# Clustered attention and experts on one core: q and k split one group sooner, masks in the order of the maxima, maxima of the second and third pair sooner

## The chip, the core and the metric

The kernel runs on one core of one Trainium2 chip. TensorE (PE in the profile) multiplies matrices, VectorE (DVE), ScalarE (ACT) and GpSimd (POOL) work on tiles, and SyncE (SP) issues nearly all DMAs. Each engine takes its own instructions in order and waits on semaphores for the others. The metric is the device time of one execution in microseconds.

## What is computed

Attention over 4 batches and 8 heads, 768 rows of 64 numbers each. Rows of q and k see each other only where their nearest of 16 centroids is the same. The result, as rows of 512 numbers, then goes through eight experts, one for each row that passes a gate.

```python
q_assign = np.argmax(np.einsum('bhsd,hcd->bhsc', q_n, c_n), axis=-1)
k_assign = np.argmax(np.einsum('bhsd,hcd->bhsc', k_n, c_n), axis=-1)
mask = q_assign[:, :, :, None] == k_assign[:, :, None, :]
scores = scale * np.matmul(q, k.transpose(0, 1, 3, 2))
scores = np.where(mask, scores, -1000000000.0)
scores = scores - np.max(scores, axis=-1, keepdims=True)
attn = np.exp(scores)
attn = attn / (np.sum(attn, axis=-1, keepdims=True) + 1e-09)
...
do_compute = skip_score > 0
xc = x[do_compute]
...
    h = np.maximum(xc[mask] @ w1[e], 0.0)
    y[mask] = gate_w[mask, None] * (h @ w2[e])
out[do_compute] = xc + y
```

## The kernel before

**Pairs and slots.** The attention works on 16 pairs of heads, one after the other. A pair has 24 slots: in each, `score` multiplies 128 rows of k with 384 rows of q for one of the two heads (a = 0 or 1) in two matmuls (L560 and L561), and ACT takes the exp into a ring of tiles PT (L563). A slot is the unit of time of the plan; slot 0 is the first product of a pair, and negative numbers lie in the pairs before it. Every six slots (a group) the products with v follow on PE (`avs`, tile av, L585). After the second group of six in each half, oT takes the result out of av, which has one buffer (L607 and L608 for the first half).

**Two precisions.** q and k are split into a high part and a low rest. `split_hi` writes the high part of q (t = 0) or k (t = 1) on ACT into a tile hi (L378; two such tiles in all, q's and k's) and copies it by DMA into QM (q) or KB (k), one for each head, three sets in turn (L381). `split_lo` subtracts it from raw, in place, on DVE (L388). `copies_hi` (L396) and `copies_lo` (L402) copy high and low parts into qc and kc, two sets in turn, for the second matmul.

**Masks.** `sims` (L438) multiplies raw with the centroids, `assign` picks the best centroid in five DVE operations on mxc, eqc, mwc and oh (L451 to L462), and `masks` turns oh into rows mk (L485) that eight small DMAs write into QM and KB below the high parts (L493): t for q or k, a for the head, hf for the half of 384 columns.

**Maxima.** Before a pair's products can start, each row's maximum is needed. `smax` runs 24 times for a pair: a matmul sm of QM and KB with their masks (L522), and a maximum on DVE into M (L524). n = 0 to 5 are head 0 of the first half of q, with both halves of k in turn; 6 to 11 are head 1; 12 to 23 the second half of q. `mneg` takes the maximum over M into MX (L535), and `mrows` turns MX on PE (L543) and writes it into QM as a row (L548).

**The order.** `steps` takes all steps of all pairs from one heap by their slot numbers and writes the instructions in that order; it sets the order on each engine's queue, not times. The numbers stand in PLAN, with FIRST in place of it for pairs 0, 1 and 2. `hi` and `lo` have two numbers, for q and k; `copies` has one for the high parts and one each for the low parts of q and k; `load` fetches raw (two buffers); `smax` is the first number, the step, and the gap between the halves (and a step for the second half where it differs); `oT` is the delay behind the last product with v of a half. A group counts six slots, so a number that falls by 6 goes one group forward, while all numbers 24 apart are at the same place of successive pairs.

**What else uses the queues.** SP also loads v (vt, L356), writes out the attention (`put_out`, out<-x, L668, behind the ACT rows of L676), and brings pieces of the experts' weights (wraw, L1040) during pairs 3 to 6. `sums`, `recip` and the routing are on PE, ACT and DVE between the slots. POOL adds up the exps (acc, L574).

Of the kernel before, what the change touches and what calls it, by code (L numbers as in the profile page):

```python
# [12 lines left out]
F32 = mybir.dt.float32  # L13
# [10 lines left out]
H, S, D, NCL = 8, 768, 64, 16  # L24
HP = H // 2
HALF = S // 2
# [17 lines left out]


PLAN = {
    "load": -54.0, "load_v": -45.0, "weights": 72.0, "sims": -42.9, "assign": (-42.45, 0.07, 0.02, 2.0, 0.02, 0.02),
    "hi": (-34.3, -28.3), "masks": (-34.5, 0.12), "lo": (-28.35, -10.35), "copies": (-23.3, -23.2, -10.3),
    "smax": (-21.1, 1.0, -0.4), "mneg": (-9.0, 3.2), "mrows": ((-4.5, 0.2, 0.05), (5.5, 0.1, 0.05)),
    "av": 1.6, "oT": (4.5, 3.55), "sums": 29.2, "recip": 31.5, "xout": (31.52, 49.55, 37.55),  # L50
    "tail": ((16.0, 16.6, 19.2), (28.5, 28.6, 29.3)),
    "route": (29.25, 34.9, 58.9), "early": (86.5, 100.9),
    "rtail": ((5.3, 10.9, 16.2, 17.5, 21.5, 18.2, 23.6, 24.2), (5.35, 10.92, 29.1, 29.2, 29.4, 29.5)),
# [6 lines left out]
FIRST = {  # L60
    0: {
        "load_v": -18.9, "sims": -20.0, "hi": (-19.9, -19.8, -19.7, -19.6), "assign": (-19.0, 0.1, 0.01, 0.01, 0.01, 0.01),
        "lo": (-18.7, -18.6, -16.9, -16.8), "masks": -17.0, "smax": (-14.0, 0.1, 13.0, 0.6), "mneg": (-12.85, 7.55),
        "mrows": ((-12.8, 0.1, 0.0), (8.2, 0.1, 0.0)),
    },
    1: {
        "sims": -42.2, "hi": (-42.4, -42.3), "lo": (-40.1, -40.0), "copies": (-39.9, -39.8, -39.7), "assign": (-36.83, 13.2, 1.3, 1.3, 1.3, 1.3),
        "masks": (-17.6, 0.1), "smax": (-14.5, 1.0, 0.0, 0.92), "mneg": (-2.3, 8.2), "mrows": ((-1.6, 0.1, 0.2), (8.8, 0.3, 0.3)),
    },
    2: {  # L70
        "load": -64.75, "smax": (-16.0, 0.95, 0.0), "mneg": (-5.2, 6.3), "mrows": ((-4.5, 0.2, 0.05), (7.4, 0.3, 0.3)),
    },
}

# [3 lines left out]
class Kernel:  # L78
# [397 lines left out]
    def masks(self, i, wait):  # L476

        c, nc = self.st[i], self.nc
        mp = self.xps([P, HALF])
        for b in range(NB):  # L480
            nc.tensor.matmul(mp[:, b * P:(b + 1) * P], lhsT=c["oh"][:, b].rearrange("p t h x -> p (t h x)"),
                             rhs=self.ident_bf, start=True, stop=True)
        yield wait
        mk = self.small.tile([P, HALF], F32R, name="mk", bufs=1)
        nc.scalar.activation(out=mk, in_=mp, func=AF.Identity, scale=self.mscale, bias=self.mbias)  # L485
        yield 0.3
        for t in range(2):
            for a in range(2):
                r = 64 + NCL * a
                for hf in range(2):  # L490
                    m0 = 64 * t + 32 * hf + NCL * a
                    dst = (c["kb"] if t else c["qm"])[a][r:r + NCL, hf * HALF:(hf + 1) * HALF]
                    nc.sync.dma_start(out=dst.bitcast(F32), in_=mk.bitcast(F32)[m0:m0 + NCL, :])  # L493

    def mask_rows(self, i, t, hf, mp):
        for b in range(NB):
# [842 lines left out]
```

## Time and profile before

| | |
|---|---|
| median of 3 runs | 740.55 us (735.31 to 742.02) |
| the profiled execution | 735.29 us, span of its instructions 733.6 us |
| attention ends, experts begin | near 505 us |
| TensorE clock granted, mean | 0.981 |
| DMAs moved | 110.16 MB, mean 150 GB/s |

The prediction quotes the profile. A line of waits has who waited and for whom, then us in total, times and the longest. A line of the timeline has start and duration in us, engine, line, operation, out<-in, the number of such instructions, and in brackets the engine's idle time before it with what ended it. A line of a stretch has its bounds and length, then for PE, PEld (weight loads), DVE, ACT and POOL the busy time with the number of instructions, then the granted share of the TensorE clock, the DMA share and GB/s. Tile names stand without their numbers, so QM is any of six. What ended a wait is inferred from semaphores; of several that a matmul waits for, the last is named.

### The profile page before, as it was taken

To read this page: it belongs to the slowest core of one execution; us is meant where nothing else is said; L and a number is where in the kernel's file an instruction comes from. 1 tells how busy PE (TensorE), PEld (TensorE's weight loads), DVE (VectorE), ACT (ScalarE), POOL (GpSimd) and SP (SyncE) were. 2 spreads that over 40 slices of the span, in tenths; PEclk is the share of its full clock that TensorE was granted. 3 is DMA by queue.
4 is the path that set the end of the run, shared out by engine and by line. 5 is a ranking of instruction groups with operands and counts; after the bars stand their busy time and mean duration, and the time that the engine had idled before them with its cause. 6 is when DMAs were issued, how large, how long until landed. Compare 5 with 4: busy or idle time off the path is not lost.

```text
span 733.6 us, 12354 instructions
## 1 busy us (share of the span) xinstructions
PE 675.4 (92%) x3961; PEld 472.0 (64%) x3961; DVE 499.8 (68%) x1022; ACT 425.7 (58%) x958; POOL 366.2 (50%) x390
## 2 busy tenths in 40 slices
PE   5798899999989989998999999998899999999995
PEld 2455556655656656565565656555578988998883
DVE  6856566757868757797675878776567876667711
ACT  6465657666656666775676757583454455455520
POOL 8664547756556665774665747642442222221001
PEclk9999999999999999999999999998799999999998
DMA  7643637575683663735646456140266666667520
GB/s 216 158 113 87 157 86 207 146 200 143 174 206 102 171 162 99 182 91 146 164 116 165 115 123 151 48 137 23 85 210 202 241 224 215 209 212 243 177 71 30
DMA packets 54353, 110.16 MB, mean 150 GB/s; under 512 B 8615, under 2 KB 22823, under 8 KB 54288
## 3 DMA queue, kind: packets, MB, share of 16 engines
q1 hardware_dynamic: 50832, 101.73, 49.9%
q0 software_dynamic: 2656, 7.24, 3.0%
q8 instruction: 32, 0.52, 0.3%
q10 hardware_dynamic: 800, 0.39, 0.2%
q14 instruction: 33, 0.27, 0.1%
HBM read 61.00 MB, written 10.62 MB: 98 GB/s over the span
## 4 chain that ended last, share of the span: by engine, by line
PE 57%; DMA 17%; issue 10%; DVE 4%; ACT 4%; POOL 3%; SPq 3%; POOLq 0%; ACTq 0%
PE av L585 13%; PE ps L560 9%; PE sm L522 8%; PE ps L561 7%; DMA out<-yo,idw 6%; DMA KB<-hi 5%; SPq L493 2%; DMA qc<-hi 2%; PE py L1070 2%; PE py L1071 2%; PE py L1072 2%; ACT PT L563 2%; DMA xg<-out,idr 2%; PE x_ps L438 2%; PE x_ps L617 2%
## 5 line engine op out<-in xcount | busy, mean ns | idle before, releaser
L574 POOL TENSOR_TENSOR acc<-acc,PT 128x384 f32<-128x384 f32 x248 | 239.7, 992 | 98.0 <-ACT PT L563 97.6
L563 ACT ACTIVATE PT<-ps 128x384 f32<-128x384 f32 x384 | 187.3, 492 | 148.8 <-PE ps L561 117.1
L524 DVE TENSOR_REDUCE M<-sm 128x1 f32<-128x384 f32 x384 | 204.2, 554 | 99.5 <-PE sm L522 98.1
L522 PE MATMUL sm<-KB,QM 96*128 96x384 f32 x384 | 138.8, 368 | 18.3 <-DMA KB<-hi 6.8
L560 PE MATMUL ps<-QM,KB 98*128 98x384 f32 x384 | 148.1, 386 | 2.8 <-ACT PT L563 1.5
L585 PE MATMUL av<-PT,vt 128*64 128x385 f32 x768 | 140.1, 500 | 3.9 <-ACT oT L608 3.9
L561 PE MATMUL ps<-qc,kc 128*128 128x384 f32 x384 | 132.3, 344 | 0.0
L560 PEld LDWEIGHTS ps<-QM,KB 98*128 98x128 f32 x384 | 73.3, 191 | 55.1 <-ACT PT L563 27.4
L522 PEld LDWEIGHTS sm<-KB,QM 96*128 96x128 f32 x384 | 75.1, 196 | 41.3 <-issue 29.2
L568 POOL TENSOR_TENSOR acc<-PT 128x384 f32<-128x384 f32 x64 | 54.3, 861 | 92.8 <-ACT PT L563 58.6
L585 PEld LDWEIGHTS av<-PT,vt 128*64 128x64 f32 x768 | 49.9, 137 | 62.2 <-issue 53.6
L966 POOL DMA_INDIRECT out<-yo,idw x15 | 19.3, 1286 | 113.5 <-DVE yo L1094 102.3
L561 PEld LDWEIGHTS ps<-qc,kc 128*128 128x128 f32 x384 | 74.3, 194 | 0.0
L1070 PE MATMUL ph<-x2l,w1h 128*128 128x256 f32 x224 | 63.6, 284 | 1.6 <-DVE x2l L1082 1.6
L1071 PE MATMUL ph<-x2h,w1h 128*128 128x256 f32 x224 | 63.6, 284 | 0.0
L1072 PE MATMUL ph<-x2h,w1l 128*128 128x256 f32 x224 | 63.5, 283 | 0.0
L1146 DVE SCALAR_TENSOR_TENSOR hl<-ph,hh 128x256 fp32r<-128x256 f32 x56 | 23.7, 423 | 38.6 <-ACT hh L1145 38.6
L1145 ACT ACTIVATE hh<-ph 128x256 fp32r<-128x256 f32 x56 | 21.5, 383 | 48.0 <-PE ph L1072 47.8
L676 ACT ACTIVATE x<-x_ps,rs 128x64 f32<-128x64 f32 x186 | 41.5, 323 | 11.2 <-DVE rs L633 7.1
L1070 PE MATMUL py<-w2l,hh 128*128 128x512 f32 x112 | 45.0, 402 | 0.0
L1070 PEld LDWEIGHTS ph<-x2l,w1h 128*128 128x128 f32 x224 | 42.9, 192 | 2.1 <-DVE x2l L1082 1.8
L1071 PE MATMUL py<-w2h,hh 128*128 128x512 f32 x112 | 43.7, 390 | 0.0
(262 smaller groups left out, 1007.2 us busy)
## 6 DMA issues: line engine op xcount, KB each, us to landing
wraw<-w SPq DMA_DIRECT2D x72, 512.0 KB, 4.6
raw<-qk SPq DMA_DIRECT2D x16, 768.0 KB, 6.1
vt<-v SPq DMA_DIRECT2D x16, 384.0 KB, 6.0
QM<-hi SPq DMA_DIRECT2D x30, 192.0 KB, 3.4
KB<-hi SPq DMA_DIRECT2D x30, 192.0 KB, 6.4
qc<-hi SPq DMA_DIRECT2D x30, 192.0 KB, 7.4
kc<-hi SPq DMA_DIRECT2D x30, 192.0 KB, 7.1
qc<-raw SPq DMA_DIRECT2D x30, 192.0 KB, 6.9
```

The costliest lines, as they stand in the source:

```text
L522: nc.tensor.matmul(sm, lhsT=c["qm"][a][0:96, j * P:(j + 1) * P], rhs=c["kb"][a][0:96, hf * HALF:(hf + 1) * HALF], start=True, stop=True)
L524: nc.vector.tensor_reduce(out=c["m"][:, j, a, hf:hf + 1], in_=sm, axis=AX.X, op=ALU.max)
L560: nc.tensor.matmul(ps, lhsT=c["kb"][a][0:98, ks], rhs=c["qm"][a][0:98, sl], start=True, stop=False)
L561: nc.tensor.matmul(ps, lhsT=c["kc"][a][:, ks], rhs=c["qc"][a][:, sl], start=False, stop=True)
L563: nc.scalar.activation(out=pt, in_=ps, func=AF.Exp, scale=D ** -0.5)
L568: nc.gpsimd.tensor_tensor(out=acc, in0=self.pt(i, s - 2)[:, :HALF], in1=pt, op=ALU.add)
L574: (nc.vector if dve else nc.gpsimd).tensor_tensor(out=acc, in0=acc, in1=pt, op=ALU.add)
L585: nc.tensor.matmul(av[a * D:(a + 1) * D, :], lhsT=c["vt"][:, kt, a * D:(a + 1) * D], rhs=self.pt(i, hf * 2 * KT + kt * 2 + a), start=(kt = ...
L676: self.nc.scalar.activation(out=c["x"][:, j, cs], in_=xp[:, n, cs], func=AF.Copy, scale=c["rs"][:, j, 2 * hp + a:2 * hp + a + 1])
L1070: nc.tensor.matmul(ps, lhsT=ah, rhs=bl, start=first, stop=False)
L1071: nc.tensor.matmul(ps, lhsT=ah, rhs=bh, start=False, stop=False)
L1072: nc.tensor.matmul(ps, lhsT=al, rhs=bh, start=False, stop=last)
```

## The change

In PLAN, for pairs 3 on (and where FIRST says nothing): the load of raw goes from -54 to -60, the split of q from -34.3 to -40.35 and of k from -28.3 to -34.25, the low part of q from -28.35 to -34.35 and of k from -10.35 to -28.35, and the copies of k's low part from -10.3 to -23.1. oT of the first half comes one slot sooner. The eight masks are written in another order. In FIRST the second half of pair 0's maxima starts 1.1 slots later, pair 1's assign runs in one go and its masks come 4 slots and its maxima 1.8 slots sooner, pair 2's maxima 1.6 slots sooner; their mneg and mrows with them. All operations and their sizes are as before.

```diff
 PLAN = {
-    "load": -54.0, "load_v": -45.0, "weights": 72.0, "sims": -42.9, "assign": (-42.45, 0.07, 0.02, 2.0, 0.02, 0.02),
-    "hi": (-34.3, -28.3), "masks": (-34.5, 0.12), "lo": (-28.35, -10.35), "copies": (-23.3, -23.2, -10.3),
+    "load": -60.0, "load_v": -45.0, "weights": 72.0, "sims": -42.9, "assign": (-42.45, 0.07, 0.02, 2.0, 0.02, 0.02),
+    "hi": (-40.35, -34.25), "masks": (-34.5, 0.12), "lo": (-34.35, -28.35), "copies": (-23.3, -23.2, -23.1),
...
-    "av": 1.6, "oT": (4.5, 3.55), "sums": 29.2, "recip": 31.5, "xout": (31.52, 49.55, 37.55),
+    "av": 1.6, "oT": (3.5, 3.55), "sums": 29.2, "recip": 31.5, "xout": (31.52, 49.55, 37.55),
...
-        "masks": (-17.6, 0.1), "smax": (-14.5, 1.0, 0.0, 0.92), "mneg": (-2.3, 8.2), "mrows": ((-1.6, 0.1, 0.2), (8.8, 0.3, 0.3)),
+        "assign": (-36.83, 12.93, 0.2, 0.2, 0.2, 0.2), "masks": (-21.6, 0.1), "smax": (-16.3, 0.95, -0.1),
+        "mneg": (-5.3, 5.9), "mrows": ((-4.5, 0.2, 0.05), (6.4, 0.1, 0.05)),
...
-        for t in range(2):
-            for a in range(2):
-                r = 64 + NCL * a
-                for hf in range(2):
-                    m0 = 64 * t + 32 * hf + NCL * a
-                    dst = (c["kb"] if t else c["qm"])[a][r:r + NCL, hf * HALF:(hf + 1) * HALF]
-                    nc.sync.dma_start(out=dst.bitcast(F32), in_=mk.bitcast(F32)[m0:m0 + NCL, :])
+
+        for t, hf, a in ((0, 0, 0), (1, 0, 0), (1, 1, 0), (0, 0, 1), (1, 0, 1), (1, 1, 1), (0, 1, 0), (0, 1, 1)):
+            r, m0 = 64 + NCL * a, 64 * t + 32 * hf + NCL * a
+            dst = (c["kb"] if t else c["qm"])[a][r:r + NCL, hf * HALF:(hf + 1) * HALF]
+            nc.sync.dma_start(out=dst.bitcast(F32), in_=mk.bitcast(F32)[m0:m0 + NCL, :])
```

What that does to the queues is shown at three places; line numbers after the change are one lower or one higher than before. First SP, where one of the later pairs (the set QM10, QM11, KB10, KB11) gets its operands. The number behind a name is that of its buffer: hi_3388 is q's high part, hi_3476 k's. Before:

```order
L668 DMA out<-x_3288 128x3x128
L402 DMA kc0_3157<-raw_2736 64x768
L402 DMA kc1_3158<-raw_2736 64x768
L381 DMA QM10_174<-hi_3388 64x768
L381 DMA QM11_175<-hi_3388 64x768
L493 DMA QM10_174<-mk_3381 16x384 x2
L493 DMA QM11_175<-mk_3381 16x384 x2
L493 DMA KB10_180<-mk_3381 16x384 x2
L493 DMA KB11_181<-mk_3381 16x384 x2
L348 DMA raw_3444<-qk 128x1536
L381 DMA KB10_180<-hi_3476 64x768
L381 DMA KB11_181<-hi_3476 64x768
```

And SP after the change for the same pair, where hi_3312 is q's high part and hi_3395 k's:

```order
L382 DMA QM10_174<-hi_3312 64x768
L382 DMA QM11_175<-hi_3312 64x768
L667 DMA out<-x_3291 128x3x128
L349 DMA raw_3370<-qk 128x1536
L382 DMA KB10_180<-hi_3395 64x768
L382 DMA KB11_181<-hi_3395 64x768
L492 DMA QM10_174<-mk_3390 16x384
L492 DMA KB10_180<-mk_3390 16x384 x2
L492 DMA QM11_175<-mk_3390 16x384
L492 DMA KB11_181<-mk_3390 16x384 x2
L492 DMA QM10_174<-mk_3390 16x384
L492 DMA QM11_175<-mk_3390 16x384
```

The copies into QM now stand ahead of out, the load and the copies into KB ahead of the masks, and the copies of the preceding pair's low part of k have left this place for one directly behind q's.

Second ACT, from the rows of out (x) of one later pair to the maxima's row of the next; PT rows are exps. Before:

```order
L676 ACTIVATE x<-x_ps,rs 128x64 x6
L563 ACTIVATE PT<-ps 128x384 x6
L485 ACTIVATE mk<-x_ps,mbias,mscale 128x384
L378 ACTIVATE hi<-raw 128x768
L563 ACTIVATE PT<-ps 128x384 x5
L607 ACTIVATE vm<-av 128x1
L608 ACTIVATE oT<-av,vm 128x384
L563 ACTIVATE PT<-ps 128x384
L378 ACTIVATE hi<-raw 128x768
L548 ACTIVATE QM_174<-x_ps 2x384
```

And ACT after the change:

```order
L675 ACTIVATE x<-x_ps,rs 128x64 x6
L379 ACTIVATE hi<-raw 128x768
L562 ACTIVATE PT<-ps 128x384 x6
L486 ACTIVATE mk<-x_ps,mbias,mscale 128x384
L379 ACTIVATE hi<-raw 128x768
L562 ACTIVATE PT<-ps 128x384 x4
L606 ACTIVATE vm<-av 128x1
L607 ACTIVATE oT<-av,vm 128x384
L562 ACTIVATE PT<-ps 128x384 x2
L547 ACTIVATE QM_174<-x_ps 2x384
```

The split of q stands behind the rows of out, that of k where q's stood, and vm and oT one exp further forward.

Third DVE in pair 1, from oT of pair 0 to the maxima of pair 1's second half (M1 belongs to pair 1, M0 here to pair 2). Before:

```order
L603 TENSOR_SCALAR oT_555<-av_625,vm_715 128x384
L451 TENSOR_REDUCE mxc_764<-x_ps_759 128x24
L454 TENSOR_TENSOR eqc_766<-x_ps_759,mxc_764 128x384
L524 TENSOR_REDUCE M1_201<-sm_768 128x1
L524 TENSOR_REDUCE M1_201<-sm_776 128x1
L633 RECIPROCAL rs_98<-x_ps_784 128x3x2 x2
L524 TENSOR_REDUCE M1_201<-sm_802 128x1
L457 TENSOR_TENSOR eqc_766<-eqc_766,wts_114 128x384
L460 TENSOR_REDUCE mwc_812<-eqc_766 128x24
L462 TENSOR_TENSOR oh_763<-wts_114,mwc_812 128x384
L524 TENSOR_REDUCE M0_200<-sm_820 128x1
L535 TENSOR_REDUCE MX1_197<-M1_201 128x3x2
```

And DVE after the change:

```order
L602 TENSOR_SCALAR oT_567<-av_641,vm_727 128x384
L523 TENSOR_REDUCE M1_201<-sm_768 128x1
L452 TENSOR_REDUCE mxc_776<-x_ps_771 128x24
L455 TENSOR_TENSOR eqc_778<-x_ps_771,mxc_776 128x384
L534 TENSOR_REDUCE MX1_197<-M1_201 128x3x2
L523 TENSOR_REDUCE M0_200<-sm_790 128x1
```

MX1 has moved ahead of the last three operations of pair 2's assign; two of them still stand between it and the last maximum.

More of the change, by code (lines that the diff above doesn't have):

```diff
@@ L62 @@
         "load_v": -18.9, "sims": -20.0, "hi": (-19.9, -19.8, -19.7, -19.6), "assign": (-19.0, 0.1, 0.01, 0.01, 0.01, 0.01),
-        "lo": (-18.7, -18.6, -16.9, -16.8), "masks": -17.0, "smax": (-14.0, 0.1, 13.0, 0.6), "mneg": (-12.85, 7.55),
+        "lo": (-18.7, -18.6, -16.9, -16.8), "masks": -17.0, "smax": (-14.0, 0.1, 14.1, 0.55), "mneg": (-12.85, 7.55),
         "mrows": ((-12.8, 0.1, 0.0), (8.2, 0.1, 0.0)),
@@ L66 @@
     1: {
-        "sims": -42.2, "hi": (-42.4, -42.3), "lo": (-40.1, -40.0), "copies": (-39.9, -39.8, -39.7), "assign": (-36.83, 13.2, 1.3, 1.3, 1.3, 1.3),
-        "masks": (-17.6, 0.1), "smax": (-14.5, 1.0, 0.0, 0.92), "mneg": (-2.3, 8.2), "mrows": ((-1.6, 0.1, 0.2), (8.8, 0.3, 0.3)),
+        "sims": -42.2, "hi": (-42.4, -42.3), "lo": (-40.1, -40.0), "copies": (-39.9, -39.8, -39.7),
+        "assign": (-36.83, 12.93, 0.2, 0.2, 0.2, 0.2), "masks": (-21.6, 0.1), "smax": (-16.3, 0.95, -0.1),
+        "mneg": (-5.3, 5.9), "mrows": ((-4.5, 0.2, 0.05), (6.4, 0.1, 0.05)),
     },
     2: {
-        "load": -64.75, "smax": (-16.0, 0.95, 0.0), "mneg": (-5.2, 6.3), "mrows": ((-4.5, 0.2, 0.05), (7.4, 0.3, 0.3)),
+        "load": -64.75, "smax": (-17.6, 0.97, 0.0), "mneg": (-6.4, 5.2),
     },
```

## The prediction

> **What bounds the kernel now.** I read the page first, then the waits of PE, then the stretches of single pairs, then SP's timeline ahead of one stall.
>
> ```profile
> span 733.6 us, 12354 instructions
> PE 675.4 (92%) x3961; PEld 472.0 (64%) x3961; DVE 499.8 (68%) x1022; ACT 425.7 (58%) x958; POOL 366.2 (50%) x390
> ```
>
> PE is busy for 675.4 of 733.6 us, so the most that any new order can win without removing matmuls is the 58 us in which it idles, and what it runs slowly. PE's own waits (us in total, times, longest) name what it idles for:
>
> ```profile
> PE sm L522 <- DMA KB<-hi: 6.8, 6, 2.3
> PE x_ps L543 <- DVE MX L535: 5.1, 5, 2.7
> PE sm L522 <- DMA qc<-hi: 4.2, 3, 1.9
> PE av L585 <- ACT oT L608: 3.9, 13, 0.6
> PE sm L522 <- issue: 2.5, 1, 2.5
> PE sm L522 <- DMA KB<-mk: 1.7, 1, 1.7
> ```
>
> The matmul of the maxima (sm, L522) reads QM and KB, never qc. The rows that name qc<-hi or issue are the same wait as KB<-hi: a pair's first maximum waits for the copy of k into KB. That is 6.8 + 4.2 + 2.5 = 13.5 us in ten stalls. Is a stall made up later? Compare one pair without and one with such a stall of 2.33 us (PE is the first engine in a row; PEclk, DMA share and GB/s are the last three numbers):
>
> ```profile
> 299.60:327.90 28.30, 27.86 (x166) 17.59 (x165) 24.79 (x54) 19.84 (x50) 18.50 (x21) 1.00 0.53 140
> 327.90:358.90 31.00, 27.99 (x165) 17.71 (x164) 24.47 (x49) 19.62 (x49) 18.50 (x21) 1.00 0.55 136
> ```
>
> PE's work is the same within 0.13 us, and the pair is 2.7 us longer. The stall is paid in full, because no other engine is full. SP's timeline shows why KB is late (start, duration):
>
> ```profile
> 251.92 0.39 SPq L668 DMA_DIRECT2D out<-x  x1
> 257.44 1.11 SPq L402 DMA_DIRECT2D kc<-raw  x2
> 258.64 1.19 SPq L381 DMA_DIRECT2D QM<-hi  x2
> 259.88 2.64 SPq L493 DMA_DIRECT2D QM<-mk  x4
> 262.56 2.48 SPq L493 DMA_DIRECT2D KB<-mk  x4
> 265.09 1.19 SPq L348 DMA_DIRECT2D raw<-qk  x1
> 266.37 1.14 SPq L381 DMA_DIRECT2D KB<-hi  x2
> ```
> ```profile
> 273.59 0.42 PE L522 MATMUL sm<-KB,QM 96*128 96x384 f32 x1 [1.56 <-DMA qc<-hi]
> ```
> ```profile
> raw<-qk SPq DMA_DIRECT2D x16, 768.0 KB, 6.1
> QM<-hi SPq DMA_DIRECT2D x30, 192.0 KB, 3.4
> KB<-hi SPq DMA_DIRECT2D x30, 192.0 KB, 6.4
> KB<-mk SPq DMA_DIRECT2D x60, 24.0 KB, 1.9
> ```
>
> SP idles for 5 us, then issues 15 DMAs back to back, and the two copies into KB stand last, behind eight masks and a 768 KB load. It lands after 6.4 us where the equal copy into QM, with no load ahead of it, takes 3.4.
>
> **The change part by part.** No operation is added or removed; only places change.
>
> *First maxima of the later pairs (13.5 us).* The split of k, its copies into KB and the load move one group forward. ACT at the same place:
>
> ```profile
> 250.56 1.34 ACT L676 ACTIVATE x<-x_ps,rs 128x64 f32<-128x64 f32 x6 [0.63 <-DVE rs L633]
> 253.30 0.87 ACT L563 ACTIVATE PT<-ps 128x384 f32<-128x384 f32 x2 [1.40 <-PE sm L522]
> 256.74 0.67 ACT L485 ACTIVATE mk<-x_ps,mbias,mscale 128x384 fp32r<-128x384 f32 x1
> 257.30 0.84 ACT L378 ACTIVATE hi<-raw 128x768 fp32r<-128x768 f32 x1
> ```
>
> The split of q (0.84 us) now follows the x rows, where ACT idles for 1.40 us: nothing is lost. SP then has two copies into QM, out and the load, and starts them at about 251.9 + 0.84 = 252.7; the load is issued by about 254.3 (1.19 + 0.39 later) and lands, at 6.1 us, near 260.4. The split of k takes the place of q's, done at 258.14, so KB is issued near 258.2 and, at QM's 3.4 us, lands near 261.6. The eight masks follow from 259.4 at (2.64 + 2.48)/8 = 0.64 us each: the first three by 261.3, landed at 1.9 us near 263.2. PE wants them at 273.59 - 1.56 = 272.0. The lead is 9 us; with KB's present 6.4 us, and the masks only behind it, about 6 us. So all 13.5 us go; the bound on the other side is 0. The copies of k's low half move two issues (1.11 us) out of this run to a place directly behind q's; vt and out leave up to 2 us later for it, vt with more than a pair's time to spare, and out is read by nobody before the experts. DVE does as many subtractions at the same places, q's where k's stood.
>
> *The half clock (5.1 us).* Behind three of the gaps PE runs at half clock for 3.4 us, busy throughout:
>
> ```profile
> 67.50:70.90 3.40, 3.40 (x12) 3.40 (x13) 1.40 (x3) 1.45 (x4) 0.86 (x1) 0.50 0.00 0
> 91.40:94.80 3.40, 3.40 (x14) 2.35 (x16) 3.15 (x7) 1.36 (x3) 1.86 (x2) 0.50 1.06 264
> 214.30:217.70 3.40, 3.40 (x18) 1.86 (x20) 2.96 (x7) 1.60 (x4) 2.69 (x3) 0.50 1.05 244
> 334.30:337.70 3.40, 3.19 (x25) 1.90 (x25) 2.74 (x6) 1.85 (x4) 1.82 (x3) 1.00 1.05 230
> ```
>
> Each of the first three does 1.7 us of work in 3.4 us, 5.1 us lost in all. The last row, behind the stall of 2.33 us, kept full clock, so a gap does not always cost this. Bounds 0 and 5.1; I take 5.1, since all three stand directly behind gaps that shrink. [...]
>
> *oT one slot earlier (3.3 us).* Before av PE waits 13 times for oT:
>
> ```profile
> 233.20 0.49 ACT L563 ACTIVATE PT<-ps 128x384 f32<-128x384 f32 x1 [0.25 <-PE ps L561]
> 233.78 0.58 ACT L608 ACTIVATE oT<-av,vm 128x384 f32<-128x384 f32 x1
> ```
> ```profile
> 234.42 0.54 PE L585 MATMUL av<-PT,vt 128*64 128x385 f32 x2 [0.27 <-ACT oT L608]
> ```
>
> oT now stands ahead of that exp of 0.49 us, more than the 0.27 us. Thirteen waits make 3.9, the longest is 0.6. I take twelve short ones, 3.3 us, and leave the long one: in that place (pair 1) the rows of the maxima now stand just ahead of av and wait for DVE instead. Bounds 0 and 3.9.
>
> *The first pairs (5.3 us).*
>
> ```profile
> 32.71 2.47 SPq L493 DMA_DIRECT2D QM<-mk  x4
> ```
> ```profile
> 23.36 0.56 DVE L524 TENSOR_REDUCE M<-sm 128x1 f32<-128x384 f32 x1 [2.07 <-PE sm L522]
> 25.23 0.55 DVE L454 TENSOR_TENSOR eqc<-x_ps,mxc 128x384 f32<-128x384 f32 x1
> ```
> ```profile
> 67.48 0.86 PE L543 MATMUL x_ps<-ident,MX 128*128 128x128 f32 x3 [2.66 <-DVE MX L535]
> 79.17 0.52 PE L543 MATMUL x_ps<-ident,MX 128*128 128x128 f32 x3 [0.42 <-DVE MX L535]
> 98.86 0.41 PE L543 MATMUL x_ps<-ident,MX 128*128 128x128 f32 x2 [1.09 <-DVE MX L535]
> ```
>
> Pair 1's clusters are now chosen in one run on DVE, from 23.36 - 2.07 = 21.3 on: five operations like the 0.55 us one above, some longer, about 3.3 us by my estimate, so that the masks leave near 26 and not at 32.71, in the order in which they are used. The 1.7 us of KB<-mk go, though its maxima start 1.8 slots sooner. PE may wait for that run of DVE; against it stands that it fills DVE's idle 2.07 us, and I count half a microsecond won. Of the 5.1 us on MX, pair 2's 0.42 and 1.09 go, since its maxima end a slot sooner. Of pair 1's 2.66, MX still stands behind two assign operations of 0.55 us, so 1.1 stays and 1.6 goes. Sum 1.7 + 0.5 + 1.5 + 1.6 = 5.3; bounds: -2 (the denser start makes PE wait for DVE) and 7.
>
> Sum: 13.5 + 5.1 + 3.3 + 5.3 = 27.2 us. The profiled execution took 735.29 us, its span 733.6 and 1.7 around it, and is the fastest of those known; the median of the three is 740.55. By the profile 735.3 - 27.2 = 708.1, by the median 713.3. The trace does not show what the slower runs lost; landings that race with PE would be one way, and these go. I take 710.
>
> **The rivals.**
>
> *Half is given back.* With PE's gaps closed, ACT and DVE have less time to catch up. For it: DVE is busy 24.79 of 28.30 us in the pair above. Against it: that pair has no stall and already runs so. Half of the 13.5 and 3.3 lost again gives 27.2 - 8.4 = 18.8: 716.5 by the profile, 722 by the median.
>
> *The clock drops stay.* Then 22.1 us are won: 713.2 by the profile, 718 by the median.
>
> *The stall changes its owner.* The masks, now last on SP, arrive as late as KB did. It takes 6 us more than worked out above; a load landing late would do it, as KB is behind it. Then 13.5 and 3.4 of the clock stay: 27.2 - 16.9 = 10.3, 725 by the profile, 730 by the median. [...]
>
> *Slower: ACT waits at the new split of q.* It writes a hi tile that the preceding pair's copies into qc still read, and it comes six slots sooner than before. ACT is in order, so exps and then PE would stand.
>
> ```profile
> DMA to landing us min/median/max: 6.3/7.1/7.6
> ```
>
> That row is of the qc and kc copies issued between 238.9 and 241.8; the two into qc (issued up to 239.6) land by 247.2, and ACT comes to the new place at 251.90: 4.7 us to spare, and after the change neither load nor KB stands ahead of these copies. It decides if they land over 4.7 us later. Thirteen pairs pay each further microsecond; 27.2/13 = 2.1 us undo the gain, and 3 us make 735.3 - 27.2 + 39 = 747.
>
> **How the numbers follow.** Forecast 0.67 (710), half given back 0.12, clock drops stay 0.12, stall changes owner 0.06, ACT waits 0.03. One per cent, about what a measurement of this kernel can tell from no change, is 7.4 us: faster is below 733.1. The first three are faster, of the fourth two thirds, which makes 0.95; I take 0.93, leaving 0.04 for no change and 0.03 slower. The range is 703 to 722: below, the early bound of 7 and all of oT (705.8) with some spread; above, the half at the median. It leaves out the last two cases and a little of each other, under 0.2.
>
> **What would show it.** L522 no longer waits for KB<-hi, qc<-hi or issue over 0.3 us; KB lands in 3 to 4 us; PEclk is 1.00 at all pairs from the third on; av waits no more for oT; one wait of about 1 us on MX is left near 65 us. Pairs without routing take 28 us throughout. I am wrong if ACT idles ahead of the first hi, if L522 waits for a mask, or if PE's waits vanish and pairs still take 30 us.

## The result, and the profile after

The changed kernel takes 707.78 us (median of four runs, 702.11 to 709.43) where the kernel before takes 738.58 us (four runs, 735.31 to 742.02). The ratio is 0.957, with a 95% interval of 0.950 to 0.964. The forecast of 710 us and its range hold it.

The head of the page of the changed kernel, and PE's waits that are left (us in total, times, longest):

```profile
span 705.3 us, 12376 instructions
PE 669.8 (95%) x3961; PEld 469.9 (67%) x3961; DVE 502.2 (71%) x1022; ACT 423.4 (60%) x958; POOL 366.3 (52%) x390
```
```profile
PE x_ps L848 <- DVE ohd L801: 3.2, 1, 3.2
PE ph L1069 <- DVE x2l L1081: 2.6, 1, 2.6
PE x_ps L888 <- DVE rhs L883: 2.6, 1, 2.6
PE x_ps L542 <- DVE MX L534: 2.3, 3, 1.2
PE sm L521 <- DVE M L523: 2.0, 2, 1.5
```

The rows of KB<-hi, qc<-hi and issue at the maxima, of KB<-mk, and of av on oT are all gone. The three largest rows shown lie in the routing of the last pair and in the experts, and stood there before (that of x2l with 1.6 us). PE works 5.6 us less (669.8 against 675.4) and idles 22.7 us less, which is the 28.3 us by which the span is shorter.

The later pairs are now even. Two stretches of a pair's length, one behind the other, have PE busy for all but 0.2 us each (bounds and length, then PE's busy time first):

```profile
271.30:299.60 28.30, 28.12 (x168) 18.08 (x168) 24.17 (x54) 20.00 (x51) 18.91 (x21) 1.00 0.55 148
299.60:327.90 28.30, 28.12 (x168) 17.93 (x166) 25.66 (x50) 20.05 (x51) 18.92 (x22) 1.00 0.56 147
```

The timeline gives SP's two issues into KB for one of them, and the first maximum that reads them (start, duration):

```profile
263.55 0.47 SPq L349 DMA_DIRECT2D raw<-qk  x1
267.59 1.11 SPq L382 DMA_DIRECT2D KB<-hi  x2
268.74 0.60 SPq L492 DMA_DIRECT2D QM<-mk  x1
```
```profile
280.97 0.34 PE L521 MATMUL sm<-KB,QM 96*128 96x384 f32 x1
```
```profile
KB<-hi SPq DMA_DIRECT2D x30, 192.0 KB, 2.9
```

From the second issue (268.1) to the maximum pass 12.9 us; the copy takes 2.9 us (median), so it lands 10 us before it is wanted. SP issues these copies at the end of ACT's split (266.72 + 0.84 = 267.56 us, the first issue at 267.59) and no longer behind eight masks.

One row is in every trace and stands late enough to split the gain: the wait of 1.5 us, early in the last pair's maxima, in which PE always waits for M. Before, and after:

```profile
471.62 0.44 PE L522 MATMUL sm<-KB,QM 96*128 96x384 f32 x1 [1.49 <-DVE M L524]
```
```profile
440.68 0.44 PE L521 MATMUL sm<-KB,QM 96*128 96x384 f32 x1 [1.49 <-DVE M L523]
```

By that point 30.9 us are won; the span shows 28.3. So, with the roundings, 2.7 us are given back behind it, in the last pair and its routing. I use this row as a mark below, since it is free of what the tail does.

### The profile page after: what moved, and what is told of

It is laid out like the page before. It is cut to its first block, busy times and chain, and to the rows that moved or that the text cites. A ratio compares the mean times of both kernels' runs of the same rounds, so it can differ in the third digit from the quotient of the medians.

```text
span 705.3 us, 12376 instructions
## 1 busy us (share of the span) xinstructions
PE 669.8 (95%) x3961; PEld 469.9 (67%) x3961; DVE 502.2 (71%) x1022; ACT 423.4 (60%) x958; POOL 366.3 (52%) x390
## 4 chain that ended last, share of the span: by engine, by line
PE 74%; issue 9%; DMA 9%; DVE 4%; ACT 2%; POOL 0%; POOLq 0%; ACTq 0%; DVEq 0%
PE av L584 19%; PE ps L559 13%; PE sm L521 10%; PE ps L560 9%; DMA out<-yo,idw 6%; PE py L1069 2%; PE py L1071 2%; PE py L1070 2%; PE x_ps L439 2%; DMA xg<-out,idr 2%; PE x_ps L653 2%; PE ph L1069 2%; PE x_ps L616 2%; PE ph L1071 2%; PE ph L1070 2%
## 5 line engine op out<-in xcount | busy, mean ns | idle before, releaser
L521 PE MATMUL sm<-KB,QM 96*128 96x384 f32 x384 | 137.0, 363 | 2.2 <-DVE M L523 2.0
L1064 DVE TENSOR_TENSOR w2l<-wraw,w2h 128x1024 fp32r<-128x1024 f32 x30 | 39.5, 1318 | 8.4 <-ACT w2h L1063 7.8
```

What stands on the lines that cost most here:

```text
L521: nc.tensor.matmul(sm, lhsT=c["qm"][a][0:96, j * P:(j + 1) * P], rhs=c["kb"][a][0:96, hf * HALF:(hf + 1) * HALF], start=True, stop=True)
```

## The experiments

The kernel before was timed with each set of runs; its medians were 739.32 us (first four kernels), 737.58 us (second four) and 738.23 us (last four). A ratio is always to the kernel before.

**1. The new numbers of load, hi, lo and copies alone, in the kernel before.**

```diff
-    "load": -54.0, ...
-    "hi": (-34.3, -28.3), "masks": (-34.5, 0.12), "lo": (-28.35, -10.35), "copies": (-23.3, -23.2, -10.3),
+    "load": -60.0, ...
+    "hi": (-40.35, -34.25), "masks": (-34.5, 0.12), "lo": (-34.35, -28.35), "copies": (-23.3, -23.2, -23.1),
```

> Only the later pairs' numbers move (load, split of q and k, low parts, copies); oT, the order of the masks and the first pairs are as before. Theory (the first maximum waits for KB, and each stall is paid in full): the waits of L522 on KB<-hi, qc<-hi and issue go (13.5 us) and with them the half clock at 91 and 214 us (3.4 us): 16.9 us faster, ratio 0.977. The wait on MX near 67 us, its half clock and the 13 waits on oT (3.9 us) stay. Rival, half given back: 8 us, ratio 0.989. Rival, the clock drops have another cause: they stay, 13.5 us, ratio 0.982.

721.77 us, 0.978 (0.971 to 0.984). No wait for KB<-hi, qc<-hi or issue is left at the first maxima; what was to stay stayed (columns as above):

```profile
PE x_ps L543 <- DVE MX L535: 4.9, 5, 2.6
PE av L585 <- ACT oT L608: 3.2, 12, 0.3
```
```profile
453.65 0.45 PE L522 MATMUL sm<-KB,QM 96*128 96x384 f32 x1 [1.48 <-DVE M L524]
```

At the mark 18.0 us are won. This part is more than half of the gain.

**2. Only the load moved, behind the copies into KB, in the kernel before.**

```diff
-    "load": -54.0,
+    "load": -52.0,
```

> One number moves: the load of raw at -52.0 instead of -54.0, which puts it behind the two copies into KB on SP and nothing else. Theory A (what delays KB is the 768 KB load ahead of it): KB is issued 0.6 us sooner and lands after 3.4 instead of 6.4 us, some 2 us before PE wants it; nearly all of the 13.5 us and the 3.4 of the clock go, about 15 us, ratio 0.98. Theory B (what delays KB is its late place on SP, behind eight masks and the late split): KB still takes over 5 us, since copies and load behind it share the DMA engines; at most 4 us, ratio 0.995 or more, and L522 still waits for KB<-hi.

739.71 us, 1.001 (0.997 to 1.005). Neither theory had it right. The waits for KB did go, but others took their place:

```profile
264.35 1.18 SPq L381 DMA_DIRECT2D KB<-hi  x2
265.56 0.59 SPq L348 DMA_DIRECT2D raw<-qk  x1
```
```profile
274.39 0.85 PE L438 MATMUL x_ps<-raw,cb 128*32 128x384 f32 x8 [2.23 <-DMA raw<-qk]
```
```profile
PE x_ps L438 <- DMA raw<-qk: 17.6, 11, 3.1
```

```profile
KB<-hi SPq DMA_DIRECT2D x30, 192.0 KB, 3.1
```

The load was directly ahead of KB on the queue and did delay it: without the load ahead, and with it directly behind, KB lands after 3.1 us (median) and not 6.4. In the trace of the kernel before, a DMA was issued on SP's queue 102 times while a load of raw was on its way, and none of them landed before that load. But the centroid products (L438) want raw almost as soon, and 13.5 us of stalls became 17.6. I read from it that in the kernel before both could not be on time, since the run of 15 DMAs began too late; that is argued here, and experiment 11 bears on it.

**3. Only FIRST (the pairs 0 to 2), in the kernel before.**

```diff
-        "masks": (-17.6, 0.1), "smax": (-14.5, 1.0, 0.0, 0.92), "mneg": (-2.3, 8.2), ...
+        "assign": (-36.83, 12.93, 0.2, 0.2, 0.2, 0.2), "masks": (-21.6, 0.1), "smax": (-16.3, 0.95, -0.1),
...
-        "load": -64.75, "smax": (-16.0, 0.95, 0.0), "mneg": (-5.2, 6.3), ...
+        "load": -64.75, "smax": (-17.6, 0.97, 0.0), "mneg": (-6.4, 5.2),
```

> Only the numbers of pairs 0, 1 and 2 move; the masks go out in the old order. Theory: 5.3 us of waits (KB<-mk, MX) and 1.7 us of half clock near 67 us go: 7 us, ratio 0.9905; about 1 us of wait on MX stays in pair 1. The waits on KB<-hi of the later pairs stay as before. Rival (the denser start makes PE wait for DVE): the waits of L522 on DVE M grow by 2 us or more and the gain is under 4 us, ratio over 0.9945.

732.47 us, 0.990 (0.987 to 0.993): by the medians 7 us, as expected. The stalls of the later pairs stay, for instance

```profile
PE sm L523 <- DMA KB<-hi: 5.9, 7, 1.3
```

and the half clock near 67 us is gone. But other stalls are followed by half clock in this trace (near 86, 209, 270 and 332 us): 20.5 us of it lie ahead of the mark, where the kernel before has 10.2. At the mark, 470.96 us, only 0.7 us are won. The 10.2 us more at half clock (granted 0.50) count as 5.1 us of work; without them it would be 5.8.

**4. Only oT one slot sooner, in the kernel before.**

```diff
-    "av": 1.6, "oT": (4.5, 3.55),
+    "av": 1.6, "oT": (3.5, 3.55),
```

> One number moves: oT of the first half a slot sooner. Theory: twelve of the thirteen waits of L585 on oT go, 3.3 us, ratio 0.9955; the wait on KB<-hi grows by nothing. Rival (the stall at the next first maximum takes it back, since KB's landing does not move with PE): the waits on oT go, but L522's waits for KB<-hi grow by about 2 to 3 us and the time is the same within 1 us.

738.68 us, 1.000 (0.996 to 1.004). The rival was right; the theory's 0.9955 lies just outside the interval. The waits of av are gone, and those at the first maxima are longer:

```profile
PE sm L522 <- DMA KB<-hi: 8.3, 7, 1.8
PE sm L522 <- DMA qc<-hi: 7.9, 4, 2.8
...
PE sm L522 <- issue: 2.9, 1, 2.9
```

8.3 + 7.9 + 2.9 = 19.1 us against 13.5: PE waits there for what it saved, which fits the rival's copy that does not land sooner, though no row here shows the landing. The 5.6 us are more than the 3.9 that were saved; this trace also has 37.5 us at half clock ahead of the mark, against 10.2, and what the rest of them is stays open.

**5. The changed kernel with the masks in their old order** (the loops over t, a, hf again).

> The changed kernel with the masks in the old order (q's four, then k's four). Theory (the masks have a lead of several us in the later pairs): the same time as the changed kernel, ratio to before 0.957 within 0.004; only in pair 1, where the maxima begin as the masks land, up to 1 us of wait. Rival (the order is what lets the maxima begin): L521 waits for KB<-mk in most pairs, 0.6 to 2 us each, 7 us or more in all, ratio 0.966 or more.

706.22 us, 0.956 (0.950 to 0.962). The order is worth nothing that can be measured: with the copies into KB landing 10 us early and the masks behind them, PE waits for no mask in either order.

**6. The changed kernel with the load later, nominally directly ahead of the copies into KB.**

```diff
-    "load": -60.0,
+    "load": -58.26,
```

> The changed kernel with the load of raw at -58.26 instead of -60, directly ahead of the copies into KB. It is held back to the place where it stood relative to KB before the change. Theory (lead of about 6 us even if KB takes 6.4 us): where SP was free the load still goes early or KB lands late, but the maxima do not wait: ratio to before 0.957 within 0.004. Rival (the stall changes its owner): L521 waits for KB<-hi or the masks by 1 us or more in most pairs, 10 us or more in all, ratio 0.97 or more.

707.15 us, 0.959 (0.953 to 0.966). This run tells nothing apart: the load already stood directly ahead of KB in most pairs, and the edit only swapped it with a piece of the experts' weights in a few. It is a repeat of the changed kernel.

**7. The changed kernel with the split of q another group sooner**, which is the mechanism of the slower rival.

```diff
-    "hi": (-40.35, -34.25),
+    "hi": (-46.35, -34.25),
```

> The changed kernel with the split of q another group sooner (-46.35), one slot behind the issue of the preceding pair's copies into qc, which read the tile that it writes. Theory of the slower case: ACT stands for these copies, some 3 to 5 us a pair, and PE loses 2 to 4 us in each of 13 pairs: 25 to 50 us slower than the changed kernel, ratio to before 0.99 to 1.03, with ACT's wait at L379 on the qc copies. Rival (nothing holds the tile so long): the time of the changed kernel, ratio 0.957.

723.46 us, 0.980 (0.973 to 0.986): 16 us lost against the changed kernel. ACT waits for the copies that still read the hi tile, and PE then waits for ACT:

```profile
ACT hi L379 <- DMA qc<-hi: 20.5, 13, 3.0
```
```profile
PE ps L559 <- ACT vm L600: 7.0, 9, 2.3
PE ps L559 <- ACT PT L562: 6.2, 9, 1.8
```

The mechanism is real and all 13 pairs have it. It costs less than the 25 to 50 us expected: ACT waits 1.6 us on average in each, and some of it lies where PE does not need ACT.

**8. The changed kernel with pair 1's rows of maxima 0.7 slots later.**

```diff
-        "mneg": (-5.3, 5.9), "mrows": ((-4.5, 0.2, 0.05), (6.4, 0.1, 0.05)),
+        "mneg": (-5.3, 5.5), "mrows": ((-4.5, 0.2, 0.05), (7.1, 0.1, 0.05)),
```

> The changed kernel with pair 1's last maximum of maxima (mneg) ahead of pair 2's assign on DVE, and its transposes one score later on PE. Theory: the wait of about 1.2 us on MX near 58 us in the changed kernel's profile falls below 0.4 us; up to 1 us faster than the changed kernel, less than a measurement can tell, ratio to before 0.956. Rival: the wait moves to another place near by (DVE's maxima late), and the span is the same.

706.21 us, 0.955 (0.949 to 0.961). The wait of 1.2 us is gone:

```profile
PE x_ps L542 <- DVE MX L534: 0.9, 2, 0.6
```

The time can't be told from that of the changed kernel.

**9. The changed kernel with oT back in its old slot (4.5).**

> The changed kernel with oT back in its old slot (4.5). Theory: once the first maxima of a pair no longer stall, the waits of the matmuls av for oT are on the path: about 12 waits and 3.3 us come back, so about 711 us, a ratio to the kernel before of about 0.962. Rival: oT's slot is worth nothing here either, as it was worth nothing when it alone was changed (1.000): the waits for oT show in the trace, but the ratio stays 0.957, within 0.002.

711.29 us, 0.964 (0.960 to 0.968). The median is 3.5 us above the changed kernel's; the intervals overlap, so the profile has to decide. It does:

```profile
PE av L584 <- ACT oT L607: 3.5, 13, 0.3
```
```profile
445.63 0.45 PE L521 MATMUL sm<-KB,QM 96*128 96x384 f32 x1 [1.48 <-DVE M L523]
```

At the mark it is 5.0 us later than the changed kernel. There six traces of the changed kernel and its neighbours (experiments 5, 6, 8, 11 and 12) all lie between 440.32 and 441.33, so 5.0 us is well outside.

**10. The new numbers of experiment 1 and oT together, in the kernel before.**

> The kernel before with the new numbers of load, hi, lo and copies (which alone gave a ratio of 0.978) and the new one of oT (which alone gave 1.000). Theory: the two together give more than their sum, since the stall that swallowed oT's gain is gone: 3.3 us less than with load, hi, lo and copies alone, about 0.973. Rival: 0.978, oT is worth nothing.

717.08 us, 0.970 (0.965 to 0.975), against 0.978 for experiment 1 and 1.000 for experiment 4. The mark:

```profile
449.64 0.44 PE L522 MATMUL sm<-KB,QM 96*128 96x384 f32 x1 [1.48 <-DVE M L524]
```

453.65 - 449.64 = 4.0 us, though the two intervals overlap. Experiments 9 and 10 agree: oT is worth 4 to 5 us once the stalls at KB are gone, and nothing while they stand.

**11. The changed kernel with the load back behind the masks (-54.0).**

> The changed kernel with load put back behind the masks (-54.0), so that on SP's queue the copies KB and the masks come first, then raw, then the copies qc. Theory: with hi and lo split a group sooner the load may come late as well as early: the ratio stays at 0.957 within 0.004, with small waits of L439 for raw at most. Rival: as when load alone was put behind the copies, raw lands too late for the sums of the later pairs: L439 waits over 1 us for it in most pairs, 10 us or more in sum, and the ratio is 0.970 or above.

707.58 us, 0.958 (0.953 to 0.963): the theory's. SP's timeline has KB first, then the masks, then the load:

```profile
267.83 1.10 SPq L382 DMA_DIRECT2D KB<-hi  x2
...
274.04 0.58 SPq L349 DMA_DIRECT2D raw<-qk  x1
...
276.44 1.14 SPq L397 DMA_DIRECT2D qc<-hi  x2
```

No matmul of L439 waits for raw. So what removes the stalls is the split of q and k one group sooner, with the low parts and copies that moved with it; these were not tried apart. Where the load stands no longer matters, within this measurement.

**12. The changed kernel with matmuls of ones, whose result nobody reads, in two waits of the last pair's routing.** 26 stand ahead of the matmul of L848 and 20 ahead of that of L888.

```diff
+    def spin(self, n):
+        t = self.ps_sm.tile([P, HALF], F32, name="sm")
+        for _ in range(n):
+            self.nc.tensor.matmul(t[:, :2 * P], lhsT=self.ones_bf, ...)
```

> The changed kernel with 46 matmuls of ones, whose result is not used, in the two places near 481 and 491 us where PE waits 2.6 and 3.2 us for the routing of the last pair. Theory: the half clock near 470 and 490 us follows those idle stretches of PE; with PE kept busy the two stretches of 6.8 us shrink or go, which gives 3 to 7 us: 0.947 to 0.953. Rival: the half clock comes there for another reason, or the added matmuls cost as much as they give: 0.957 or above.

704.84 us, 0.955 (0.951 to 0.960), between the two expectations: 2.9 us below the changed kernel's median, which the intervals can't tell from nothing. Its span is 701.8 us. In the profile half clock fell from 17.1 us between 470 and 525 us to 6.8 us; the next section shows that only 3.4 us of that can be laid to these matmuls.

## Why the prediction was right, point by point

**First maxima of the later pairs (13.5 us).** Right, in size and mechanism. Experiment 1 won 18.0 us at the mark, where 13.5 and two of the three clock drops (3.4) were forecast for it. Its trace lost these two drops but has a new one near 30 us, so 16.3 of the 18.0 us are not the clock; they hold the 13.5, and shorter waits for oT, masks and exps (3.9 to 3.2, 1.7 to 0.9 and 1.5 to 0.7 us). For KB the working gives a lead of 10.4 us (272.0 - 261.6), and 10 were measured. The working treated the load as the cause of KB's 6.4 us; experiments 2 and 11 show it as half the story, since the load can't simply step aside, and needn't once the splits are sooner.

**oT (3.3 us).** The size was nearly right, at 4.0 and 5.0 us where 3.3 was forecast, but the sum took the term as one that adds to the others, and it does not: alone it is worth 1.000. Nothing in the forecast showed this, because it came only for the whole change.

**The first pairs (5.3 us).** Right in size. Experiment 3 gave 7 us by the medians, as expected of 5.3 and one clock drop of 1.7; its trace has the 5.3 (5.8 without the clock) and more half clock, not less. In the changed kernel the mark comes 9.0 us sooner than in experiment 10, which lacks FIRST and the order of masks. Experiment 10 has two clock drops ahead of the mark, at 30 and 68 us, the changed kernel none; that is 3.4 us, and leaves 5.5. Pair 1's masks leave at 25.64 us, where 26 was worked out. Of MX, 1.19 us was left in pair 1 where 1.1 was forecast (at 58.8 us, not 65):

```profile
58.80 0.52 PE L542 MATMUL x_ps<-ident,MX 128*128 128x128 f32 x3 [1.19 <-DVE MX L534]
```

**The half clock (5.1 us).** All three stretches went, and each with its gap: those at 91 and 214 us in experiment 1, which leaves the gap and the stretch at 68; that one in experiment 3. In the changed kernel no half clock is left from 25 us to the last pair. The rival by which the drops stay is out. The forecast could not explain a stall of 2.33 us without a drop; the traces show in what it differs from the others. In all 14 traces the granted clock changes only on a fixed grid of 3.413 us, to within 2 ns: 67.5, 91.4 and 214.3 in the kernel before, where it goes from 1.00 to 0.50, are 7 and 36 such steps apart. Here are single steps of that grid in the kernel before (bounds and length, busy times, granted clock third from last): two that end at a drop, then the two that share the stall of 2.33 us.

```profile
87.98:91.40 3.42, 1.49 (x9) 1.20 (x8) 0.86 (x2) 0.55 (x2) 0.86 (x1) 1.00 1.05 225
210.86:214.28 3.42, 0.88 (x6) 0.81 (x5) 0.33 (x1) 0.55 (x2) 0.86 (x1) 1.00 1.02 207
...
330.33:333.74 3.41, 1.84 (x10) 0.58 (x6) 1.27 (x4) 1.13 (x5) 0.86 (x1) 1.00 1.01 248
333.74:337.16 3.42, 2.65 (x21) 1.85 (x25) 2.20 (x6) 1.48 (x3) 1.28 (x2) 1.00 1.05 228
```

PE idled 1.93 and 2.54 us in the first two steps. The stall near 334 lies across a boundary, 1.6 us on one side and 0.8 on the other, and no drop follows. Over all traces, of the steps at full clock between 25 and 685 us, 39 have 1.9 us or more of idle PE, and half clock follows every one; seven of them, with 1.93 to 2.66 us, are in the traces of the kernel before and of the changed one. Of 34 steps with 1.4 to 1.9 us it follows 16, and none of the three in these two traces (1.57, 1.59 and 1.64 us). Below 1.4 us it begins behind 15, in these two traces behind 2 of 362, with 0.3 us each; 14 of the 15 are one case that stays open (below). By these counts the 1.6 us could have gone either way; that 2.33 us in one step would have been followed by half clock is my estimate from the 39 of 39.

The same bears on the tail. The changed kernel's waits of 2.57 and 3.20 us in the last routing, by steps:

```profile
480.46:483.88 3.42, 1.78 (x13) 0.92 (x15) 2.94 (x15) 0.00 (x0) 0.70 (x1) 1.00 0.01 2
487.29:490.71 3.42, 1.30 (x6) 0.72 (x4) 3.25 (x6) 3.42 (x9) 2.77 (x2) 1.00 0.42 117
490.71:497.53 6.82, 5.74 (x20) 4.25 (x21) 3.77 (x17) 1.27 (x3) 0.99 (x1) 0.50 0.35 124
```

The second wait puts 2.1 of its 3.20 us into one step and is followed by half clock (0.50 from 490.71 us); in experiment 9 the boundaries cut the same two waits so that no step has 1.9 us of idle PE, and neither is:

```profile
485.19:488.61 3.42, 1.56 (x12) 0.78 (x14) 2.94 (x15) 0.00 (x0) 0.92 (x1) 1.00 0.01 2
492.02:495.43 3.41, 1.52 (x7) 0.90 (x5) 3.20 (x7) 3.41 (x9) 2.76 (x2) 1.00 0.30 74
```

Between 25 and 530 us it has 6.8 us at half clock where the changed kernel has 17.1, which is 5.1 us of work. So its span (706.2 us) is only 0.9 us above the changed kernel's although it is 5.0 us behind at the mark. In experiment 12 the first wait was covered but for 0.4 us, and 2.0 us of the second were left; the stretch behind the second shrank from 6.8 to 3.4 us. The rest of what its trace has less is not the added matmuls' doing: the stretch near 470 us stands ahead of them, and is 3.4 us in experiment 11 too; that near 521 us is gone in experiment 6 too, where the wait for x2l ahead of it is 1.6 us as here.

One drop per trace stays open: the one that begins at 470.2 us in the changed kernel, with only 0.3 us of idle in the step ahead of it. It stands at the same place of the program in all 14 traces, in experiment 12 too. In each of them that step holds twelve matmuls of a single column, which count as 1.4 us of PE's busy time:

```profile
468.31 1.39 PE L640 MATMUL sm<-ones,acc 128*128 128x1 f32 x12
```

Counted as idle they bring the step to 1.32 to 1.39 us. Twelve more like them come 16 us later; in ten of the traces they fill a step that has 1.29 us by this count, and no drop follows. The drop follows 1.32 to 1.39 us and not 1.29, but steps with 1.4 to 1.9 us fall both ways, and no run separates the two: the cause is not shown. The forecast that the clock is full in every pair from the third on failed there, in the last pair.

**Half is given back.** It was not: 30.9 us were won at the mark against a sum of 27.2. In the tail 2.7 us went the other way. One of them is the wait for x2l in the experts, 2.6 us where it was 1.6; the other 1.7 are half clock (17.1 us of it where there were 13.7), whose last stretch, near 521 us, stands directly behind that wait. It need not be a price of the change: in experiment 6, which is the changed kernel but for a few swaps, the wait is 1.6 us, that stretch is absent, and 0.2 us are given back.

**The stall changes its owner** did not happen either, but experiment 2 shows that it is what happens when only the load is moved. That no mask passes KB holds in the traces: a DMA was issued on SP's queue while a copy into KB was on its way 190 times in that of the kernel before and 142 times in that of experiment 6, and none landed before it.

**ACT waits at the new split of q** was rightly a small chance: it takes one more group (experiment 7, where ACT waits 20.5 us in 13 waits).

The steps to the mark are 18.0 us (experiment 1), 4.0 (oT on top) and 9.0 (FIRST and the order of masks on top). Each is taken from the one before, so that they make the 30.9 by construction; what they test is each term. Without the half clock they are 16.3, 4.0 and 5.5, or 25.8 us, where the forecast has 13.5, 3.3 and 5.3, or 22.1. So 3.7 us more than forecast were won ahead of the mark, and 2.7 us that the forecast did not have were lost behind it. That the spans differ by 28.3 us where the sum was 27.2 is in part luck: the two errors cancel. The range of the forecast was wide enough for what single runs do.

## What to carry to other kernels

Here several small DMAs of one queue shared one late start. Moving one of them behind another moved the stall with it (13.5 us at KB became 17.6 at raw in experiment 2); starting the run sooner, at its producer, won 18.0 us (experiment 1), and the order within it stopped mattering (706.22 and 707.58 us in experiments 5 and 11, against 707.78). So look at the start of a run before its order. The saving at oT, on PE, which next waits for a copy, was worth nothing until that copy was early (1.000 in experiment 4, 4.0 and 5.0 us in experiments 10 and 9), so test such a saving on top of the removed stall, not alone. And ask of a gap on PE not only how long it is but how the grid of the clock cuts it: behind the same wait of 3.2 us (L848) the changed kernel, with 2.12 us of idle PE in one step, has 6.8 us at half clock, and experiment 9, with 1.89 us, has none.

## What the hardware showed unexpectedly

The grid is fixed within an execution but lies at another place in each: from the start of the span, its steps begin at 2.65 us and multiples of 3.413 us behind it in the kernel before, at 2.59 in the changed kernel, at 0.50 in experiment 9. So behind the same gap (3.2 us at L848) the changed kernel has 6.8 us at half clock and experiment 9 has none. That fits a good part of the scatter: of the changed kernel and its neighbours, whose marks agree within 1.0 us, the span is 701.8 us with 6.8 us of half clock between 25 and 530 us (experiment 12), 703.0 with 13.7 (experiment 6), 705.3 with 17.1 (the changed kernel), 706.2 with 17.1 (experiment 11), 707.5 with 20.5 (experiment 5) and 706.4 with 23.9 (experiment 8).
